# Attention with a cumulative bias and two mixers on one core: queries and keys of batches 1 to 3 split in place instead of through HBM

## The chip, the cores and the metric

The kernel runs on one core of a Trainium2 chip. The metric is the device time of one execution in microseconds (us). TensorE (PE) does the matmuls, VectorE (DVE), ScalarE (ACT) and GpSimd (POOL) work elementwise, SyncE (SP) issues most DMAs; each engine takes its instructions strictly in the order in which they are written, and waits at one whose operands are not there yet.

## The reference, cut to what matters

```python
# q, k, v: (4 batches, 8 heads, 576, 64); s: (4, 8, 576)
scores = q @ k.T / 8
cum    = cumsum(maximum(s, 0))
scores = where(causal, -1e9, scores + minimum(-(cum[:, None] - cum[None, :]), 0))
attn   = softmax(scores)
x      = attn @ v                       # heads side by side: (4, 576, 512)
# mixer 1: two mixes of x with the row before it (mu_k, mu_r)
y      = sigmoid(xr @ w_r) * (relu(xk @ w_k) ** 2 @ w_v)
# mixer 2: over tokens, then over channels
u      = y + (relu(y.T @ w_tok1) @ w_tok2).T
out    = u + relu(u @ w_ch1) @ w_ch2
```

The weights are float64 in memory. Where precision matters, a float32 number is held as a high part (rounded for the fast float32 matmul, `F32R`) and a low part (the rest), and a product is built from high·high, high·low and low·high.

## The kernel before, in words

The 32 (batch, head) pairs are numbered `g`. The eight of batch 0 go a short way: `early` (the first 256 rows) and `late` (the other 320) compute scores in plain float32, beside the conversion of the first weights. The 24 of batches 1 to 3 are the *visits* `i` = 0 to 23. A visit has score tiles `j` of 128 rows; the last 64 rows of an even visit and of the odd one after it share one *joint tile* of 128 rows (`scores` with `pair`), computed with the even visit's `j` = 4 and fed by the X tiles of both. So an even visit has five tiles, an odd one four.

For each tile: PE computes scores (L307, L308), DVE adds the mask and takes the maximum (L278), ACT the exponential and its sum (L289), POOL and DVE the reciprocal (L290, L291), POOL scales the tile (L292), PE transposes it (L435, L450), ACT and DVE split that into high and low (`PF`, `PT`), and PE multiplies with the values (L493).

The scores come from two matmuls of 128 contracted rows. `X1` holds four rows of bias (cumulative sums in parts), zeros, and the high parts of queries and keys in rows 64 to 127; `X2` holds low queries over high keys and high queries over low keys. There are two `X1` and two `X2`, for even and odd visits. `place(i)` fills them when visit `i`-1 begins, by four DMAs from HBM: the bias from `ext_d`, three slices from `hl_d`. The parts in `hl_d` are made two visits (128 partitions) at a time: `load` brings a quarter (queries or keys, 288 columns) into `PB`, `split` takes the high part on ACT (L75), the low part on POOL (L239), and stores both to `hl_d` (L240). `hl_d` has room for all 24 visits, `PB` for two quarters.

The bias parts are made once, at the start, in three column pieces (`split_bias`): POOL writes ones (L197) into a tile `e`, DVE fills the rest (L77, L199, L79), ACT's queue stores it to `ext_d` (L202). The pool `cp` has one buffer for `e`. Batch 0's `late_load` (L371, L372) reads `ext_d` too.

The order of instructions on each engine is laid down when the program is built: every piece of work gets a place in one line by `at(...)`, and a scheduler with a cost model takes what is ready and stands first. Units of the two mixers stand between the attention items, so PE has their matmuls between score tiles. The last 300 us are matmuls of the channel mixer.

Of the kernel before, what the change touches and what calls it, by code (L numbers as in the profile page):

```python
# [8 lines left out]
F32 = mybir.dt.float32  # L9
F32R = mybir.dt.float32r  # L10
# [9 lines left out]
def f32(ap):  # L20
    return ap.bitcast(F32)
# [3 lines left out]
def attention_moe_mixer(  # L25
# [70 lines left out]
    act = {}  # L96

    ext_d = dram.tile([G, 4, 2, S], F32, name="ext_d")
    hl_d = dram.tile([G - H, D, 4, S], F32, name="hl_d")
    y_d = dram.tile([B, DM, S], F32, name="y_d")  # L100
    u_d = dram.tile([B, DM, S], F32, name="u_d")

# [17 lines left out]
        ps_v = att.enter_context(tc.tile_pool(name="ps_v", bufs=1, space=PSUM, reuse_waits="tile"))  # L120

    VS = v_p.tile([128, NS, 2 * D], F32, name="VS")
    maskp = v_p.tile([128, S // 2], BF16, name="maskp")

# [19 lines left out]
    def constants():  # L146
        nc.gpsimd.affine_select(
            out=maskc[:, 512:640], in_=maskc[:, 512:640], pattern=[[-1, 128]],
            compare_op=ALU.is_ge, fill=-8.0e9, base=0, channel_multiplier=1,
        )  # L150
        make_identity(nc, ident)
        nc.gpsimd.memset(maskp, 0.0)
        nc.gpsimd.tensor_copy(maskp[0:TAIL, S // 2 - TAIL:], maskc[0:TAIL, 512:512 + TAIL])
        nc.scalar.dma_start(out=maskp[TAIL:2 * TAIL, S // 2 - TAIL:], in_=maskc[0:TAIL, 512:512 + TAIL])

    def behind(p, cell):
        nc.gpsimd.tensor_copy(cell, xt[0, p][0:1, 1:2])
# [13 lines left out]
    def bias_rows(cp):  # L171
# [14 lines left out]
                copy("D", e32[:, 1, 0, :], cum[:, a:z], -1.0)  # L186
        return cum, e32

    def split_bias(cp, cum, behind):
        n = 3  # L190
        for c in range(n):
            a, z = S * c // n, S * (c + 1) // n
            e = cp.tile([G, 4, 2, z - a], F32R, name="e")
            if c == 0:
                nc.gpsimd.tensor_copy(f32(e[0:1, 0, 1, 0:1]), behind)
            for r, t in ((1, 1), (3, 1), (0, 0), (2, 0)):
                nc.gpsimd.memset(f32(e[:, r, t, :]), 1.0)  # L197
            copy("D", e[:, 0, 1, :], cum[:, a:z])
            nc.vector.tensor_tensor(out=e[:, 2, 1, :], in0=cum[:, a:z], in1=f32(e[:, 0, 1, :]), op=ALU.subtract)  # L199
            for x in (0, 2):  # L200
                copy("D", e[:, x + 1, 0, :], f32(e[:, x, 1, :]), -1.0)
            nc.scalar.dma_start(out=ext_d[:, :, :, a:z], in_=f32(e))  # L202
# [10 lines left out]
    def xs(i):  # L213
        return X1[i % 2], X2[i % 2]

    qk_raw = {}

    def stage():
        if "PB" not in act:
            act["PB"] = qk_p.tile([128, 8 * QC], F32, tag="HX", name="PB")  # L220
        return act["PB"]

    def part(y):
        x, c = divmod(y, 2)
        return x, S * c // 2, S * (c + 1) // 2

    def load(i, y):
        g = visits[i][0]
        x, c0, c1 = part(y)
        t = qk_raw[i, y] = stage()[:, y % 2 * S // 2:(y % 2 + 1) * S // 2]  # L230
        nc.sync.dma_start(out=t, in_=qk[g:g + 2, :, x, c0:c1].rearrange("h d s -> (h d) s"))

    def split(i, y):
        g = visits[i][0] - H
        x, c0, c1 = part(y)
        t = qk_raw.pop((i, y))
        e = stage()[:, S + y % 2 * S:S + y % 2 * S + S].rearrange("p (t s) -> p t s", t=2)
        copy("A", e[:, 1].bitcast(F32R), t)
        nc.gpsimd.tensor_tensor(out=e[:, 0], in0=t, in1=e[:, 1], op=ALU.subtract)  # L239
        nc.sync.dma_start(out=hl_d[g:g + 2, :, 2 * x:2 * x + 2, c0:c1].rearrange("h d t s -> (h d) t s"), in_=e)  # L240

    def load_v(i):
        b, h = divmod(visits[i][0], H)
# [15 lines left out]

    def place(i):  # L260
        g = visits[i][0]
        t = hl_d[g - H]
        if i < 2:
            X2[i] = x_tile(2 + i, F32R)
        x1, x2 = xs(i)
        nc.sync.dma_start(out=f32(x1[0:4]), in_=ext_d[g])
        nc.sync.dma_start(out=f32(x1[64:128]), in_=t[:, 1:4:2])
        nc.sync.dma_start(out=f32(x2[0:64]), in_=t[:, 0:4:3])
        nc.sync.dma_start(out=f32(x2[64:128]), in_=t[:, 1:3])

    pst = {}

# [21 lines left out]
    def scores(i, j):  # L294
        pair = j == NS - 1
        w = 128 * j + (TAIL if pair else 128)
        m = 128
        q0 = 128 * j
        P = p_p.tile([128, w], F32, tag=f"P{j}", name=f"P{j}")
        mx = st_p.tile([128, 2], F32, tag="mx", name="mx")  # L300
        parts = [(0, w // 2), (w // 2, w)] if pair else [(0, w)]
        for x, (c0, c1) in enumerate(parts):
            ps = ps_s.tile([128, 512], F32, tag="s", name="s")
            for e in (1, 0) if pair else (0,):
                x1, x2 = xs(i + e)
                n, a = (TAIL * (1 + e), S - TAIL * (1 + e)) if pair else (128, q0)
                nc.tensor.matmul(ps[0:n, 0:c1 - c0], x1[:, 0, a:a + n], x1[:, 1, c0:c1], start=True, stop=False)  # L307
                nc.tensor.matmul(ps[0:n, 0:c1 - c0], x2[:, 0, a:a + n], x2[:, 1, c0:c1], start=False, stop=True)  # L308
            softmax_max(j, ps, P, mx, x, c0, c1, None if not pair else maskp if x else maskc[:, 0:c1])
        softmax(j, P, mx, x, pair)  # L310
        pst[i, j] = P
# [20 lines left out]
    def early(h, j, V0, cp):  # L332
# [6 lines left out]
        softmax_max(j, ps, P, mx, 0, 0, w)  # L339
        softmax(j, P, mx, 0)  # L340
        if h == 0 and j == 0:
            with at(2):
                split_bias(cp, cum, P[0:1, 0:1])
        if j == 0:
            pt[0] = ps_t.tile([128, 512], F32, tag="t", name="t")
# [299 lines left out]
    def attention_item(n):  # L645
        if n < N1:
# [4 lines left out]
            if j == 2 and h > 1 and h % 2 == 0 and h // 2 + 1 < H // 2:  # L651
                with at(N0 + n):
                    late_values(h // 2 + 1)
            if h >= H - 4:
                x = 3 * (h - H + 4) + j - 2
                with at(N0 + n + 0.1):
                    if x >= 4 and x < 8:
                        split(0, x - 4)
                    if x in (2, 3, 4, 5):
                        load(0, x - 2)  # L660
                    if x == 8:
                        load_v(0)
                    if x in (10, 11):
                        load(2, x - 10)
            if h == H - 1 and j == 3:
                with at(N0 + n + 0.2):
                    split_v(0)
            if h == H - 2 and j == 2:
                with at(N0 + n):
                    for x in range(2):  # L670
                        X1[x] = x_tile(x, F32R)
                        nc.gpsimd.memset(f32(X1[x][0:64]), 0.0)
            if h == H - 1 and j == 2:
                with at(N0 + n):
                    place(0)
# [8 lines left out]
        if j == 0 and i + 1 < len(visits):  # L684
            with at(N0 + n):
                place(i + 1)
        if i % 2 == 0:
            with at(N0 + n + 0.1):
                if j < 4 and i + 2 < len(visits):
                    split(i + 2, j)  # L690
                    if j < 2:
                        load(i + 2, 2 + j)
                if j == NS - 1 and i + 2 < len(visits):
                    load_v(i + 2)
        else:
            with at(N0 + n + 0.1):
                if 2 <= j < 4 and i + 3 < len(visits):
                    load(i + 3, j - 2)
            if j == 1 and i + 1 < len(visits):
                with at(N0 + n + 0.2):  # L700
                    split_v(i + 1)
        with at(N0 + n):
            scores(i, j)
        with at(N0 + n + 1.5):
# [37 lines left out]

    act["mt"], act["mtb"], act["mtw"] = cp, 1, QC
    constants()
    with at(3):
        mixes()
    for h in range(H):
# [276 lines left out]
```

## Time and profile before

| | us |
|---|---|
| median of the runs (lowest, highest of 3) | 874.16 (873.43, 876.98) |
| the profiled execution | 872.61 |
| its span, first to last instruction | 870.8 |
| PE busy in the span | 840.6 (97%) |
| DVE, ACT, POOL busy | 485.1, 452.6, 343.4 |
| moved by DMA | 108.36 MB |

Matmul records overlap (one lasts about 0.3 us and the next starts 0.1 to 0.2 us after it), so a busy PE is not one at its peak; its waits, and the starts of successive matmuls, tell what it loses. Idle time of another engine counts only where PE waits for its result. Stretches are named by their bounds in us from the span's start.

### The profile page before, as it was taken

The page shows a single profiled execution, that of the slowest core. Times are in us where ns is not written, and L with a number is a line of the kernel's source. Part 1 is how long each engine was busy: PE and PEld are TensorE (multiplying, and loading weights), DVE is VectorE, ACT ScalarE, POOL GpSimd, SP SyncE. Part 2 cuts the span into 40 slices and gives each one's busy share as a digit, 9 for nine tenths or more (in the row PEclk, how much of TensorE's full clock was granted, in tenths as well). Part 3 has the DMA queues.
Part 4 walks back from the last instruction along what each step waited for, and adds up shares of the span by engine and source line. Part 5 has one row for each costly group of instructions (what it writes and reads, how often), then busy time and mean ns, then how long its engine had stood idle before and what let it go on. Part 6 is the DMA issues. An engine that isn't in the chain of part 4 may idle for free. (4 is left out here: it accounts for less than half of the span.)

```text
span 870.8 us, 17455 instructions
## 1 busy us (share of the span) xinstructions
PE 840.6 (97%) x6127; PEld 790.5 (91%) x6127; DVE 485.1 (56%) x1352; ACT 452.6 (52%) x1257; POOL 343.4 (39%) x601
## 2 busy tenths in 40 slices
PE   8889998999899999999999999999999999999998
PEld 5656777988789999999999989999999999999998
DVE  5797776565879566985469757951331222222221
ACT  4688766865886656868377865840310221211210
POOL 4565666864785544645256854720000000000000
PEclk9899999999999999999999999999999999999999
DMA  7943778687974244431234746553021112112100
GB/s 191 266 134 88 199 218 230 192 240 210 252 204 133 70 111 117 100 93 41 83 94 129 230 143 217 177 181 94 7 92 54 44 31 74 42 32 73 38 25 26
DMA packets 88024, 108.36 MB, mean 124 GB/s; under 512 B 11152, under 2 KB 71568, under 8 KB 87936
## 3 DMA queue, kind: packets, MB, share of 16 engines
q1 hardware_dynamic: 81408, 91.56, 37.7%
q0 software_dynamic: 4576, 15.08, 5.5%
q8 instruction: 49, 0.80, 0.4%
q10 hardware_dynamic: 1952, 0.60, 0.3%
q14 instruction: 39, 0.32, 0.1%
HBM read 77.74 MB, written 28.90 MB: 122 GB/s over the span
## 5 line engine op out<-in xcount | busy, mean ns | idle before, releaser
L863 ACT ACTIVATE HID<-c 128x256 fp32r<-128x256 f32 (+1 forms) x96 | 39.3, 410 | 220.9 <-PE c L108 220.8
L108 PE MATMUL vd<-KK,WV 128*128 128x256 f32 (+1 forms) x768 | 120.9, 300 | 0.1
L108 PEld LDWEIGHTS vd<-KK,WV 128*128 128x128 f32 x768 | 106.6, 188 | 2.4 <-issue 0.9
L292 POOL TENSOR_SCALAR P<-P,sum 128x128 f32<-128x128 f32 (+4 forms) x148 | 93.6, 636 | 36.2 <-DVE sum L291 30.2
L108 PE MATMUL h<-XK,WK 128*128 128x320 f32 (+1 forms) x672 | 105.9, 303 | 0.7 <-DVE XK L517 0.5
L108 PE MATMUL c<-HID,WV 128*128 128x256 f32 (+1 forms) x768 | 104.9, 291 | 0.0
L108 PE MATMUL c<-U,WK 128*128 128x256 f32 (+1 forms) x768 | 103.2, 291 | 1.4 <-DVE HID L864 1.4
L289 ACT ACTIVATE P<-P,mx 128x128 f32<-128x128 f32 (+4 forms) x148 | 86.9, 588 | 30.3 <-DVE mx L278 23.0
L108 PEld LDWEIGHTS c<-HID,WV 128*128 128x128 f32 x768 | 100.6, 188 | 0.0
L108 PEld LDWEIGHTS c<-U,WK 128*128 128x128 f32 x768 | 98.6, 188 | 1.7 <-DVE HID L864 1.7
L108 PEld LDWEIGHTS h<-XK,WK 128*128 128x128 f32 x672 | 93.8, 189 | 2.1 <-DVE XK L517 0.7
L864 DVE SCALAR_TENSOR_TENSOR HID<-c,HID 128x256 fp32r<-128x256 f32 (+1 forms) x96 | 43.8, 456 | 81.1 <-ACT HID L863 81.0
L278 DVE CUSTOM_DVE_ANT_0 P<-s,maskc 128x128 f32<-128x128 f32 (+4 forms) x148 | 69.1, 478 | 22.1 <-PE t L435 8.4
L928 DVE TENSOR_TENSOR ut<-c,ut 128x256 f32<-128x256 f32 (+1 forms) x32 | 14.6, 458 | 119.3 <-PE c L108 112.0
L529 POOL TENSOR_TENSOR KK<-k,KK 128x256 fp32r<-128x256 f32 (+1 forms) x64 | 55.8, 877 | 19.8 <-ACT k L528 18.7
L108 PE MATMUL r<-XR,WR 128*128 128x320 f32 (+1 forms) x384 | 60.0, 299 | 0.0
L290 POOL TENSOR_SCALAR sum<-sum 128x1 f32<-128x1 f32 (+1 forms) x148 | 32.4, 219 | 67.6 <-ACT P L289 57.2
L108 PE MATMUL c<-HID,WR 128*128 128x256 f32 (+1 forms) x384 | 54.8, 291 | 0.0
L108 PEld LDWEIGHTS r<-XR,WR 128*128 128x128 f32 x384 | 52.8, 188 | 1.1 <-ACT raw L614 0.4
L108 PE MATMUL c<-U,C1A 128*128 128x256 f32 (+1 forms) x384 | 52.8, 296 | 0.1
L108 PEld LDWEIGHTS c<-U,C1A 128*128 128x128 f32 x384 | 51.5, 190 | 0.3 <-ACT U L913 0.3
L108 PEld LDWEIGHTS c<-HID,WR 128*128 128x128 f32 x384 | 51.3, 188 | 0.0
(133 smaller groups left out, 1658.4 us busy)
## 6 DMA issues: line engine op xcount, KB each, us to landing
X<-hl_d SPq DMA_DIRECT2D x72, 288.0 KB
hl_d<-PB SPq DMA_DIRECT2D x48, 288.0 KB
raw<-in_moe_w_ch_dram POOLq DMA_DIRECT2D x48, 256.0 KB, 3.3
PB<-in_qk_dram SPq DMA_DIRECT2D x48, 144.0 KB
yt<-y_d SPq DMA_DIRECT2D x16, 288.0 KB
u_d<-yt SPq DMA_DIRECT2D x16, 288.0 KB
raw<-in_moe_w_k_dram SPq DMA_DIRECT2D x8, 512.0 KB
raw<-in_moe_w_v_dram SPq DMA_DIRECT2D x16, 256.0 KB
```

Of the source, the lines that this page charges most:

```text
L108: nc.tensor.matmul(ps, a, b, start=first and i == 0, stop=last and i == n - 1)
L278: nc.vector.tensor_tensor_reduce(out=P[0:m, c0:c1], in0=ps[0:m, 0:c1 - c0], in1=mask[0:m], scale=-scale, scalar=3.0e38 if x == 0 else mx[0 ...
L289: nc.scalar.activation(out=P[0:m, 0:w], in_=P[0:m, 0:w], func=AF.Exp, bias=mx[0:m, x:x + 1], scale=-1.0, accum_out=sm[0:m, 0:1])
L290: nc.gpsimd.tensor_scalar(out=sm[0:m, 0:1], in0=sm[0:m, 0:1], scalar1=1e-9, scalar2=1.0, op0=ALU.add, op1=ALU.mult)
L292: nc.gpsimd.tensor_scalar(out=P[0:m, 0:w], in0=P[0:m, 0:w], scalar1=sm[0:m, 1:2], scalar2=1.0, op0=ALU.mult, op1=ALU.mult)
L529: nc.gpsimd.tensor_tensor(out=kk[:, 1, m, 0:n], in0=t[:, 0:n], in1=f32(kk[:, 0, m, 0:n]), op=ALU.subtract)
L863: nc.scalar.activation(out=hi, in_=ps, func=AF.Relu)
L864: nc.vector.scalar_tensor_tensor(out=lo, in0=ps, scalar=0.0, in1=f32(hi), op0=ALU.max, op1=ALU.subtract)
L928: nc.vector.tensor_tensor(out=t, in0=ps, in1=t, op=ALU.add)
```

## The change

`hl_d` and `PB` go. `load(i)` brings queries and keys of one visit (64 partitions by 2 by 576) into a half of a tile `RQ`, the even visits into the lower 64 partitions, the odd ones into the upper; `sides(i)` says which. `place(i)` then makes all parts where they are used: for keys, then queries, ACT writes the high part into `X1`, a DMA copies it within SBUF to its place in `X2`, and POOL writes the low part into `X2` in two halves of 288 columns. It ends with the load for visit `i`+2. For odd visits the halves of X are exchanged, so that ACT and POOL stay in the same partitions.

The joint tile's columns are cut at 512 (512 and 64) instead of 288 and 288, and its mask has 64 columns. The three bias pieces get three homes (two in the tiles that later hold transposed scores, one in `cp`), their ones are written by `bias_ones` among the first instructions, and `split_bias` stands earlier in the line (`at(4)`).

```diff
-    maskp = v_p.tile([128, S // 2], BF16, name="maskp")
+    maskp = v_p.tile([128, TAIL], BF16, name="maskp")
...
+    def bias_ones(cp, n):
+        for c in range(n):
+            w = S // n
+            e = pt_tile(c, F32R)[0:G, 0:8 * w] if c < 2 else cp.tile([G, 8 * w], F32R, name="e")
+            e = e.rearrange("g (r t s) -> g r t s", r=4, t=2)
+            for r, t in ((1, 1), (3, 1), (0, 0), (2, 0)):
+                nc.gpsimd.memset(f32(e[:, r, t, :]), 1.0)
+            ones.append(e)
...
     def split_bias(cp, cum, behind):
-        n = 3
+        n = len(ones)
         for c in range(n):
             a, z = S * c // n, S * (c + 1) // n
-            e = cp.tile([G, 4, 2, z - a], F32R, name="e")
-            if c == 0:
-                nc.gpsimd.tensor_copy(f32(e[0:1, 0, 1, 0:1]), behind)
-            for r, t in ((1, 1), (3, 1), (0, 0), (2, 0)):
-                nc.gpsimd.memset(f32(e[:, r, t, :]), 1.0)
+            e = ones[c]
+            nc.gpsimd.tensor_copy(f32(e[0:1, 0, 1, 0:1]), behind)
...
+    def sides(i):
+        a, z = slice(0, D), slice(D, 2 * D)
+        return (a, z) if i % 2 == 0 else (z, a)
+
+    def raw_qk():
+        if "RQ" not in act:
+            act["RQ"] = qk_p.tile([128, 8 * QC], F32, tag="HX", name="RQ")
+        return act["RQ"][:, 0:2 * S].rearrange("p (t s) -> p t s", t=2)
+
+    def load(i):
+        nc.sync.dma_start(out=raw_qk()[sides(i)[0]], in_=qk[visits[i][0]])
...
     def place(i):
...
-        nc.sync.dma_start(out=f32(x1[0:4]), in_=ext_d[g])
-        nc.sync.dma_start(out=f32(x1[64:128]), in_=t[:, 1:4:2])
-        nc.sync.dma_start(out=f32(x2[0:64]), in_=t[:, 0:4:3])
-        nc.sync.dma_start(out=f32(x2[64:128]), in_=t[:, 1:3])
+        a, z = sides(i)
+        rq = raw_qk()[a]
+        nc.sync.dma_start(out=f32(x1[z][0:4]), in_=ext_d[g])
+        for y in (1, 0):
+            nc.scalar.activation(out=x1[a, y], in_=rq[:, y], func=AF.Copy)
+            high, low = (z, a) if y else (a, z)
+            nc.sync.dma_start(out=f32(x2[high, y]), in_=f32(x1[a, y]))
+            for c in range(2):
+                cs = slice(S * c // 2, S * (c + 1) // 2)
+                nc.gpsimd.tensor_tensor(out=x2[low, y, cs], in0=rq[:, y, cs], in1=f32(x1[a, y, cs]), op=ALU.subtract)
+        if i + 2 < len(visits):
+            load(i + 2)
...
-        parts = [(0, w // 2), (w // 2, w)] if pair else [(0, w)]
+        parts = [(0, 128 * j), (128 * j, w)] if pair else [(0, w)]
...
-            with at(2):
+            with at(4):
                 split_bias(cp, cum, P[0:1, 0:1])
```

The program's order moves with it. On POOL, at the start, the bias pieces' ones (`L197`, into `e`) stood between the first softmax tiles `P` and the first weights `WK`:

```order
L290 TENSOR_SCALAR sum<-sum 128x1
L197 MEMSET e 32x192 x4
L292 TENSOR_SCALAR P_288<-P_288,sum 128x128
L290 TENSOR_SCALAR sum<-sum 128x1
L621 TENSOR_TENSOR WK<-raw,WK 128x4x128
L292 TENSOR_SCALAR P_305<-P_305,sum 128x256
L290 TENSOR_SCALAR sum<-sum 128x1
L292 TENSOR_SCALAR P_327<-P_327,sum 128x128
L290 TENSOR_SCALAR sum<-sum 128x1
L292 TENSOR_SCALAR P_344<-P_344,sum 128x256
L197 MEMSET e 32x192 x4
```

In the changed kernel POOL reaches the same tiles with the ones long written (they are among its first rows), and only three one-element copies (L204) stand between the first tiles:

```order
L290 TENSOR_SCALAR sum<-sum 128x1
L292 TENSOR_SCALAR P_179<-P_179,sum 128x128
L290 TENSOR_SCALAR sum<-sum 128x1
L204 COPY PT_161<-P_179 1x1
L204 COPY PT_166<-P_179 1x1
L204 COPY e<-P_179 1x1
L290 TENSOR_SCALAR sum<-sum 128x1
L292 TENSOR_SCALAR P_214<-P_214,sum 128x256
L290 TENSOR_SCALAR sum<-sum 128x1
L292 TENSOR_SCALAR P_248<-P_248,sum 128x128
```

So no write of ones waits for a store of `e` in the middle of the softmax rows any more. Next, POOL at the first visits, before: single subtractions for `PB` (later visits' parts) stand between the scalings of the score tiles `P` of visits 0 and 1:

```order
L292 TENSOR_SCALAR P_1727<-P_1727,sum 128x128
L239 TENSOR_TENSOR PB<-PB 128x288
L290 TENSOR_SCALAR sum<-sum 128x1
L239 TENSOR_TENSOR PB<-PB 128x288
L290 TENSOR_SCALAR sum<-sum 128x1
L292 TENSOR_SCALAR P_1744<-P_1744,sum 128x256
L292 TENSOR_SCALAR P_1791<-P_1791,sum 128x384
L290 TENSOR_SCALAR sum<-sum 128x1
L292 TENSOR_SCALAR P_1831<-P_1831,sum 128x512
L239 TENSOR_TENSOR PB<-PB 128x288
```

In the changed kernel the same place has four subtractions together, into the `X2` of the next even visit, right behind the tiles of visit 0:

```order
L292 TENSOR_SCALAR P_1777<-P_1777,sum 128x384
L290 TENSOR_SCALAR sum<-sum 128x1
L292 TENSOR_SCALAR P_1814<-P_1814,sum 128x512
L267 TENSOR_TENSOR X_1563<-RQ,X_1459 64x288 x4
L251 TENSOR_TENSOR VV_1922<-VS,VV_1922 128x2x128
L290 TENSOR_SCALAR sum<-sum 128x1
L251 TENSOR_TENSOR VV_1922<-VS,VV_1922 128x3x128
L290 TENSOR_SCALAR sum<-sum 128x1
L267 TENSOR_TENSOR X_1709<-RQ,X_1461 64x288 x4
```

The subtractions now belong to the visit that needs them next, and come in blocks of four. Last, PE at the joint tile of visits 8 and 9 (`X_1469`, `X_1471` are the two `X1` before, `X_1576`, `X_1718` the two `X2`); before:

```order
L307 MATMUL s<-X_1471 128x288
L308 MATMUL s<-X_1718 128x288
L307 MATMUL s<-X_1469 64x288
L308 MATMUL s<-X_1576 64x288
L307 MATMUL s<-X_1471 128x288
L308 MATMUL s<-X_1718 128x288
L307 MATMUL s<-X_1469 64x288
L308 MATMUL s<-X_1576 64x288
```

and in the changed kernel (`X_1461` and `X_1709` belong to the odd visit, `X_1459` and `X_1563` to the even one):

```order
L307 MATMUL s<-X_1461 128x512
L308 MATMUL s<-X_1709 128x512
L307 MATMUL s<-X_1459 64x512
L308 MATMUL s<-X_1563 64x512
L435 MATMUL t<-ident,P_2888 128x128 x3
L493 MATMUL pv<-PF,VV_1922 128x256 x2
L493 MATMUL pv<-PF,VV_1922 128x128 x2
L435 MATMUL t<-ident,P_2923 128x128 x4
L307 MATMUL s<-X_1461 128x64
L308 MATMUL s<-X_1709 128x64
L307 MATMUL s<-X_1459 64x64
L308 MATMUL s<-X_1563 64x64
```

Four matmuls of 512 columns and four of 64 take the place of eight of 288.

## Rows read from the trace of the kernel before

**Rows 1.** Windows: us; PE, PEld, DVE, ACT, POOL busy (x); clock; DMA share; GB/s.

```profile
0.00:61.50 61.50, 52.43 (x285) 37.42 (x285) 43.91 (x132) 41.53 (x104) 34.40 (x75) 0.92 0.78 198
128.90:260.00 131.10, 119.81 (x829) 109.73 (x828) 87.60 (x299) 94.97 (x272) 89.78 (x168) 0.99 0.81 223
140.00:160.00 20.00, 17.58 (x109) 15.78 (x108) 12.58 (x43) 14.52 (x42) 14.12 (x26) 0.91 0.82 214
260.00:420.00 160.00, 159.92 (x1222) 157.79 (x1221) 116.18 (x364) 112.61 (x307) 84.34 (x161) 1.00 0.35 91
```

**Rows 2.** Waits of PE, 128.9:260 (total us, times, longest); then the longest, timeline.

```profile
PE s L308 <- DMA X<-hl_d: 4.1, 3, 2.3
...
147.07 0.30 PE L308 MATMUL s<-X 128*128 128x128 f32 x1 [2.31 <-DMA X<-hl_d]
```

**Rows 3.** Waits of ACT and of POOL, 128.9:260.

```profile
ACT PB L75 <- DMA PB<-in_qk_dram: 25.6, 17, 3.6
...
POOL PB L239 <- ACT PB L75: 16.5, 12, 3.2
```

**Rows 4.** DMA issues, 128.9:260 (count, KB each).

```profile
DMA packets 23739, 29.21 MB, mean 223 GB/s; under 512 B 2116, under 2 KB 19780, under 8 KB 23723
...
X<-hl_d SPq DMA_DIRECT2D x36, 288.0 KB
hl_d<-PB SPq DMA_DIRECT2D x34, 288.0 KB
PB<-in_qk_dram SPq DMA_DIRECT2D x34, 144.0 KB
```

**Rows 5.** Timeline of the start (start us, us, instruction, [idle before <-releaser]).

```profile
27.05 0.25 DVE L77 CAST e<-st 32x192 fp32r<-32x192 f32 x1 [2.02 <-DMA ext_d<-e]
...
27.14 0.95 POOL L197 MEMSET e<- 32x192 f32 x4 [3.40 <-DMA ext_d<-e]
...
33.12 0.40 ACT L289 ACTIVATE P<-P,mx 128x128 f32<-128x128 f32 x1 [4.00 <-DVE t L514]
```

**Rows 6.** Timeline of PE at a joint tile and behind it.

```profile
225.77 0.39 PE L308 MATMUL s<-X 128*128 128x512 f32 x1
226.00 0.29 PE L307 MATMUL s<-X 128*128 128x288 f32 x1
...
227.05 0.60 PE L435 MATMUL t<-ident,P 128*128 128x128 f32 x4
...
231.76 0.81 PE L435 MATMUL t<-ident,P 128*128 128x128 f32 x5
232.32 1.38 PE L493 MATMUL pv<-PT,VV 128*128 128x320 f32 x9
233.54 0.31 PE L307 MATMUL s<-X 128*128 128x128 f32 x1
```

**Rows 7.** Groups by shape: busy us, mean ns.

```profile
L239 POOL TENSOR_TENSOR PB<-PB 128x288 f32<-128x288 f32 x48 | 40.0, 835 | 23.9 <-ACT PB L75 18.6 <-DMA y_d<-e 3.7 <-DVE sum L291 0.6
L75 ACT ACTIVATE PB<-PB 128x288 fp32r<-128x288 f32 x48 | 21.2, 441 | 30.7 <-DMA PB<-in_qk_dram 29.8 <-POOL PB L239 0.3 <-issue 0.2
L75 ACT ACTIVATE WK<-raw 128x512 fp32r<-128x512 f32 x8 | 5.4, 677 | 1.3 <-DVE raw L616 1.3
L289 ACT ACTIVATE P<-P,mx 128x576 f32<-128x576 f32 x12 | 9.3, 773 | 4.9 <-DVE mx L278 4.7
L292 POOL TENSOR_SCALAR P<-P,sum 128x576 f32<-128x576 f32 x12 | 10.3, 856 | 1.9 <-DVE sum L291 1.8
L292 POOL TENSOR_SCALAR P<-P,sum 64x576 f32<-64x576 f32 x8 | 6.8, 846 | 3.0 <-DVE sum L291 2.9
```

**Rows 8.** DMA issues, whole span: median us from issue to landing.

```profile
raw<-in_moe_w_ch_dram POOLq DMA_DIRECT2D x48, 256.0 KB, 3.3
...
raw<-in_moe_w_tok_dram POOLq DMA_DIRECT2D x2, 128.0 KB, 2.6
```

**Rows 9.** Instructions on the tile PB: ns min/median/max, first and last start.

```profile
L239 POOL TENSOR_TENSOR PB<-PB x48: 788/810/1083, 91.3 to 267.4; 128x288 f32<-128x288 f32 x48
```

More of the change, by code (lines that the diff above doesn't have):

```diff
@@ L98, in attention_moe_mixer @@
     ext_d = dram.tile([G, 4, 2, S], F32, name="ext_d")
-    hl_d = dram.tile([G - H, D, 4, S], F32, name="hl_d")
     y_d = dram.tile([B, DM, S], F32, name="y_d")
@@ L152, in constants @@
         nc.gpsimd.memset(maskp, 0.0)
-        nc.gpsimd.tensor_copy(maskp[0:TAIL, S // 2 - TAIL:], maskc[0:TAIL, 512:512 + TAIL])
-        nc.scalar.dma_start(out=maskp[TAIL:2 * TAIL, S // 2 - TAIL:], in_=maskc[0:TAIL, 512:512 + TAIL])
+        nc.gpsimd.tensor_copy(maskp[0:TAIL], maskc[0:TAIL, 512:512 + TAIL])
+        nc.scalar.dma_start(out=maskp[TAIL:2 * TAIL], in_=maskc[0:TAIL, 512:512 + TAIL])
     def behind(p, cell):
@@ L187, in bias_rows @@
         return cum, e32
+    def bias_ones(cp, n):
[6 more added lines that the diff above has]
+            ones.append(e)
+    ones = []
     def split_bias(cp, cum, behind):
-        n = 3
+        n = len(ones)
         for c in range(n):
             a, z = S * c // n, S * (c + 1) // n
-            e = cp.tile([G, 4, 2, z - a], F32R, name="e")
-            if c == 0:
-                nc.gpsimd.tensor_copy(f32(e[0:1, 0, 1, 0:1]), behind)
-            for r, t in ((1, 1), (3, 1), (0, 0), (2, 0)):
-                nc.gpsimd.memset(f32(e[:, r, t, :]), 1.0)
+            e = ones[c]
+            nc.gpsimd.tensor_copy(f32(e[0:1, 0, 1, 0:1]), behind)
             copy("D", e[:, 0, 1, :], cum[:, a:z])
@@ L214, in xs @@
         return X1[i % 2], X2[i % 2]
[L216 to L240, printed above, removed]
+    def sides(i):
[7 more added lines that the diff above has]
+        nc.sync.dma_start(out=raw_qk()[sides(i)[0]], in_=qk[visits[i][0]])
     def load_v(i):
@@ L261, in place @@
         g = visits[i][0]
-        t = hl_d[g - H]
         if i < 2:
@@ L653, in attention_item @@
                     late_values(h // 2 + 1)
-            if h >= H - 4:
-                x = 3 * (h - H + 4) + j - 2
+            if h == H - 3 and j == 2:
                 with at(N0 + n + 0.1):
[L657 to L664, printed above, removed]
+                    load(0)
+                    load(1)
+            if h == H - 2 and j == 4:
+                with at(N0 + n + 0.1):
+                    load_v(0)
             if h == H - 1 and j == 3:
@@ L671, in attention_item @@
                         X1[x] = x_tile(x, F32R)
-                        nc.gpsimd.memset(f32(X1[x][0:64]), 0.0)
+                        nc.gpsimd.memset(f32(X1[x][sides(x)[1]]), 0.0)
             if h == H - 1 and j == 2:
@@ L686, in attention_item @@
                 place(i + 1)
-        if i % 2 == 0:
+        if i % 2 == 0 and j == NS - 1 and i + 2 < len(visits):
             with at(N0 + n + 0.1):
[L689 to L701, printed above, removed]
+                load_v(i + 2)
+        if i % 2 and j == 1 and i + 1 < len(visits):
+            with at(N0 + n + 0.2):
+                split_v(i + 1)
         with at(N0 + n):
@@ L744, in attention_moe_mixer @@
     constants()
+    bias_ones(cp, 3)
     with at(3):
```

## The prediction

> **What bounds the kernel now.** I read the busy time by stretches first. In the last 300 us and in most of the middle the starts of PE's matmuls follow one another without a gap; 260 to 420 is such a stretch: PE is idle for 0.08 of 160 us [rows 1]. There an edit helps only if it takes matmuls away, and this one doesn't. Two stretches are different. The start, 0 to 61.5, ends when the first conversions and batch 0 are done; its PE work is partly filler, so its length is set by DVE, ACT, POOL and the DMAs of the first weights (share 0.78 [rows 1]). And in 128.9 to 260, where about the first half of the visits lies, PE is busy for 119.81 of 131.10 us: it loses 11.3 us [rows 1].
>
> The views of waits say what ends those losses. 4.1 us in three waits are the second score matmul (L308) waiting for parts from `hl_d`; the longest, 2.31, ends at 147.07 [rows 2]. The window around it, 140 to 160, has a mean granted clock of 0.91 against 1.00 in 260 to 420 [rows 1]: the clock stood for part of it at 1.2 GHz instead of 2.4, after PE had been idle, and 0.09 × 20 = 1.8 us went with that. The other 7.2 us of the loss are many short waits of PE on DVE, ACT and POOL. Behind them stand longer ones: ACT waits 25.6 us for `PB` to arrive (17 times), and POOL 16.5 us for ACT's high part of it (12 times) [rows 3]. While ACT stands at L75, the exponentials behind it stand too. The DMAs behind that are 34 loads of 144 KB, 34 stores of 288 KB and 36 reloads of 288 KB, 25.7 of the 29.21 MB of the stretch [rows 4], at a DMA share of 0.81 [rows 1].
>
> **The start.** Before, the single buffer `e` makes DVE wait 2.02 and POOL 3.40 us for the store to `ext_d`, with four ones-writes of 0.95 behind it on POOL; ACT's next exponential begins only after 4.00 us of idleness [rows 5]. With three homes and early ones all this goes. Not all of ACT's 4.00 reaches the end of the start, since weights and ACT's conversions wait for DMAs too. Bounds: 0 (the weights set the end) and −5 (all of ACT's wait, and a ones-write of 0.95 more). I take −3.0, nearer to ACT's row, because the softmax items of batch 0 are one chain through ACT, DVE and POOL.
>
> **The reloads.** X no longer comes from `hl_d`: −4.1 of waits, and −1.8 of clock if nothing takes their place. I take −5.9; the smaller end is −2, if other waits keep the clock low and half of the idle time stays.
>
> **The other waits of that stretch.** ACT and POOL lose the waits at the head of their queue. The new ACT copies read a tile `RQ` loaded two visits ahead, and the stretch's traffic falls to 29.2 − 25.7 + 12 visits × (288 + 2 × 144 KB, 7.1 MB) = 10.6 MB, so the share to about 0.3. Bounds −7.2 and 0; I take half, −3.5, since half of PE's 7.2 is the plain latency of the softmax chain, which the change leaves alone.
>
> **The new chain of a visit.** A copy of 64 × 576 on ACT has no row. 128 × 288 takes 441 ns and 128 × 512 takes 677 [rows 7], which makes 0.74 at 576 columns; 64 partitions instead of 128 save nothing (846 against 856 ns on POOL at 576 columns [rows 7]). Four subtractions take 4 × 0.835 = 3.34 [rows 7]. A DMA within SBUF has no row either; 128 KB land 2.6 us after issue and 256 KB after 3.3 [rows 8], so 144 KB take about 2.7. From the moment the places in X are free, keys' copy 0.74, then POOL's 3.34 from there (queries' copy lies beside it) and some 0.8 of hand-over: 4.9 us. The DMA path, 0.74 × 2 + 2.7 + 0.4 = 4.6, lies beside that.
>
> What is there to hold it? At visits 8 and 9 the joint tile's matmuls end with the first transposes at 227.05, and the next even visit's matmul starts at 233.54 [rows 6]: a window of 6.5, less some 0.2 until the last matmul is drained. So 4.9 fits. But place's instructions stand in their queue behind what is there: with one exponential (0.77), one scaling (0.86) and one 0.835 of another unit ahead [rows 7], it is 7.4, 1.1 us late. Before, a reload of 288 KB was late at three visits [rows 2]. For odd visits the window is longer, as four of five tiles lie in it. I take 1.1 late at about half of the six even visits of the stretch: +3. Bounds: 0, if POOL is free each time, and +11, if 1.8 is lost at each of six. Behind a late subtraction on POOL stand the scalings, then PE's transposes.
>
> **Joint tiles.** Before, eight matmuls of 288 columns start from 226.00 to 227.05, 0.131 each. 512 columns take 0.23 (225.77 to 226.00), and small ones, by the five transposes from 231.76 to 232.32, 0.112 each [rows 6]. If a 64-column one is bound by its weight load as these are, the new tile takes 4 × 0.23 + 4 × 0.112 = 1.37 against 1.05; if it is bound by columns, 4 × 0.23 + 4 × 0.03 = 1.04. I take 1.26, so +0.21 for each of 12, +2.5. Bounds 0 and +3.8.
>
> **More work on POOL and ACT.** POOL has 96 subtractions instead of 48 (+40 us), ACT 48 copies of 0.74 for 48 of 0.441 (+14) [rows 7], as 64 partitions are done at a time. In 128.9 to 260 POOL comes to 89.8 − 34 × 0.835 + 48 × 0.835 = 101.5 of 131, ACT to 95.0 − 15.0 + 17.9 = 97.9. In 260 to 420, where nearly all splits were already done, POOL goes from 84.3 to about 118 of 160 and ACT from 112.6 to about 127 [rows 1]. That PE was idle for 0.08 there shows slack of unknown depth. Bounds 0 and +8 (a loss per time as in the stretch before); I take +2. The cover is the mixer units between score tiles; if it is gone, rival 2 has the price.
>
> **Sum.** −3.0 − 5.9 − 3.5 + 3 + 2.5 + 2 = −4.9. From the profiled execution's 872.6 that is 867.7; the median of the runs, 874.16, lies 1.55 above that execution, so 869.3.
>
> **Rivals.**
>
> 1. The stretch becomes as smooth as 260 to 420. For it speaks that there, with loads and splits nearly over and the share at 0.35, PE lost 0.08 [rows 1]; against it, that in that stretch POOL had a third less to do. −3 − 11.3 − 1.8 + 2.5 = −13.6, so 860.5.
>
> 2. The split is late at every even visit. Mechanism: place(i) can't start until the even X is free, at the end of the joint tile, and its four subtractions end last; the even visit's L308 waits, and PE's order lets nothing past it. At 1.5 late for 11 placed even visits it costs 16.5 and the clock's 1.8 comes back, on top of the joint tiles' 2.5, while start and reloads give −3 − 5.9: 872.6 + 11.9, so with the 1.55 some 886 (884 to 886 as the lows come out). It decides from 0.7 us per even visit: the forecast's sum without its +3 is −7.9, and 7.9 / 11 = 0.7 takes all of it; from (7.9 + 4.4) / 11 = 1.1 the kernel is slower by more than noise. For it speaks the small margin of 6.3 over 4.9, against it that mixer units can be ordered ahead of the score tile. What POOL's instructions cost beside a busy DVE bears on this: L239 ran 48 times with 788 at least, 810 as the median and 1083 ns at most [rows 9], so a wait for DVE was 0.27 us at worst. The Trainium skill ("SBUF — State Buffer", section "Who interferes with whom") says that a DVE instruction with two SBUF inputs and a GpSimd one that reads SBUF shut each other out for the whole instruction, which speaks against twice as many subtractions; by that rule four of them could be 4 × 0.27 = 1.1 us later (an estimate from rows 9). The trace shows it at few of the 48, as the median lies 22 ns above the least.
>
> 3. Nothing is left. The start's end is set by the first weights' DMAs (share 0.78 [rows 1]), which is unchanged, so its −3 goes; and late splits eat what the reloads gave. −5.9 − 3.5 + 3 + 2.5 + 2 and 3 more of late splits = +1, some 875.
>
> **How the numbers follow.** Forecast 0.45, rival 1 0.20, rival 2 0.20, rival 3 0.15. About 0.5% (4.4 us) is what a measurement of this kernel can tell from no change: faster means below 869.8, slower above 878.5. The forecast's own range is 865 to 875, just over half of it below 869.8 by its terms' bounds; with rival 1 that makes 0.44 faster. Rival 2 and a thin end of the forecast give 0.22 slower, the rest, with rival 3, 0.34. The range: 860 takes in most of rival 1 (its better half lies beyond), 882 the half of rival 2 with lateness near 1.1; some 0.2 stay outside.
>
> **What would show it.** The first `h` matmuls 3 us earlier and no wait of DVE or POOL on `ext_d<-e`: the start. No releaser `hl_d` in PE's waits and a clock of 1.00 from 140 to 160: the reloads. ACT's 25.6 gone and PE's loss in the stretch of the visits near 6: the other waits. PE waiting at L308 on POOL's L267 for about 1 us at some even visits: the chain; at all of them: rival 2. Starts of the 64-column matmuls 0.03 or 0.11 apart: the joint tile. The forecast is wrong if the stretch's loss stays above 11 us, or if 260 to 420 shows idle time of PE of several us.

## The result: slower by 0.8%, and the profile after

The changed kernel takes 883.12 us (median of 7 runs, 879.6 to 886.7) against 876.27 of the kernel before on the same chip (7 runs, 873.43 to 878.11). The ratio is 1.0083 with a 95% interval of 1.0061 to 1.0105. That is slower, and above the predicted range. The profiled execution took 883.61 us, its span is 881.8.

The stretches of the changed kernel, in the columns of [rows 1] (length; busy us and count of PE, PEld, DVE, ACT and POOL; granted clock; DMA share; GB/s):

```profile
0.00:61.50 61.50, 49.96 (x289) 35.47 (x289) 42.91 (x129) 40.97 (x101) 35.30 (x80) 0.97 0.83 203
60.00:75.00 15.00, 11.52 (x45) 7.03 (x44) 12.23 (x29) 9.69 (x26) 7.73 (x10) 0.66 0.18 54
128.90:260.00 131.10, 122.07 (x831) 110.22 (x830) 88.18 (x288) 96.98 (x255) 99.17 (x175) 0.97 0.31 77
140.00:160.00 20.00, 16.68 (x96) 13.67 (x95) 11.15 (x33) 13.23 (x32) 16.11 (x26) 0.91 0.31 78
260.00:420.00 160.00, 156.31 (x1179) 151.12 (x1178) 119.69 (x355) 120.08 (x319) 121.55 (x204) 1.00 0.25 66
```

Read three things in it. The DMA share of 128.9 to 260 fell as forecast (0.81 to 0.31). POOL's busy time rose as forecast, to 99 and 122. But PE, idle for 0.08 us in 260 to 420 before, now loses 3.69 there, and the clock is low in a place where it was not before, at 60 to 75 (0.66; 1.00 before). Equal windows do not hold quite the same work: the first score matmul of a visit starts at 135.2, where it started at 128.8 before.

Where PE waits now, over the whole span (us in total, times, longest):

```profile
PE pv L360 <- ACT T L75: 5.3, 3, 2.7
PE s L307 <- DVE mx L278: 5.2, 7, 2.4
PE s L392 <- DVE mx L278: 4.9, 2, 3.5
```

No wait on `hl_d` is left; the waits of [rows 2] are gone. In their place score matmuls (L307 of the visits, L392 of batch 0) wait for DVE's maximum of an earlier tile, which has to free a score buffer; the waits at L360 belong to the start. The longest on a visit ends at 152.55, almost where the old one ended (147.07). The timeline around it:

```profile
149.41 3.56 POOL L267 TENSOR_TENSOR X<-RQ,X 64x288 fp32r<-64x288 f32 x4 [0.97 <-ACT X L262]
...
149.54 2.02 DVE L515 SCALAR_TENSOR_TENSOR t<-xt,omu,t 128x320 f32<-128x320 f32 x2
...
151.82 0.67 DVE L278 CUSTOM_DVE_ANT_0 P<-s,maskc 128x512 f32<-128x512 f32 x1
...
152.55 0.44 PE L307 MATMUL s<-X 128*128 128x384 f32 x1 [2.38 <-DVE mx L278]
```

While POOL runs its four subtractions for the next visit, two instructions of DVE take 2.02 us together. One of this shape takes 0.54 elsewhere in the same trace (383.06, below). PE stands for 2.38 us until the maximum behind them is there. About 1 us of that is the slowness of the two; the rest is the plain order of DVE's instructions (the same place without POOL's reads is shown below, with the fill).

```profile
383.06 0.54 DVE L515 SCALAR_TENSOR_TENSOR t<-xt,omu,t 128x320 f32<-128x320 f32 x1
```

To count such losses I took windows of 5 us from 60 to 610 in each trace, and summed PE's idle time and, for the clock, 5 us times what the granted clock lacks to 1.00. Before: 17.8 idle and 1.7 clock. After: 22.1 and 8.6. The two make 11.2 us more, and the span is 11.0 longer. So the lower clock behind the waits is the larger part in these windows of this execution. The start, which they leave out, went the other way: its clock rose from 0.92 to 0.97, and PE's idle time in 0 to 61.5 from 9.07 to 11.54. The medians, 6.9 us apart, say that this pair of executions shows more than the usual difference.

### The profile page after: what moved, and what is told of

Same layout as the page of the kernel before. It is cut to its first block, busy times and chain, and to the rows that moved or that the text cites. A ratio compares the mean times of both kernels' runs of the same rounds, so it can differ in the third digit from the quotient of the medians.

```text
span 881.8 us, 17430 instructions
## 1 busy us (share of the span) xinstructions
PE 846.1 (96%) x6127; PEld 790.1 (90%) x6127; DVE 493.0 (56%) x1352; ACT 466.4 (53%) x1257; POOL 386.9 (44%) x651
## 5 line engine op out<-in xcount | busy, mean ns | idle before, releaser
L107 PE MATMUL vd<-KK,WV 128*128 128x256 f32 (+1 forms) x768 | 118.6, 300 | 0.0
L292 POOL TENSOR_SCALAR P<-P,sum 128x128 f32<-128x128 f32 (+4 forms) x148 | 95.4, 650 | 36.7 <-DVE sum L291 28.7
L289 ACT ACTIVATE P<-P,mx 128x128 f32<-128x128 f32 (+4 forms) x148 | 86.6, 586 | 28.7 <-DVE mx L278 24.3
L278 DVE CUSTOM_DVE_ANT_0 P<-s,maskc 128x128 f32<-128x128 f32 (+4 forms) x148 | 72.0, 497 | 38.6 <-PE t L435 20.2
L267 POOL TENSOR_TENSOR X<-RQ,X 64x288 fp32r<-64x288 f32 x96 | 80.8, 860 | 12.6 <-ACT X L262 8.0
L615 DVE SCALAR_TENSOR_TENSOR raw<-raw 128x256 int32<-128x256 int32 (+2 forms) x77 | 39.8, 519 | 22.4 <-ACT raw L614 15.0
```

The source lines that it names most:

```text
L107: nc.tensor.matmul(ps, a, b, start=first and i == 0, stop=last and i == n - 1)
L267: nc.gpsimd.tensor_tensor(out=x2[low, y, cs], in0=rq[:, y, cs], in1=f32(x1[a, y, cs]), op=ALU.subtract)
L278: nc.vector.tensor_tensor_reduce(out=P[0:m, c0:c1], in0=ps[0:m, 0:c1 - c0], in1=mask[0:m], scale=-scale, scalar=3.0e38 if x == 0 else mx[0 ...
L289: nc.scalar.activation(out=P[0:m, 0:w], in_=P[0:m, 0:w], func=AF.Exp, bias=mx[0:m, x:x + 1], scale=-1.0, accum_out=sm[0:m, 0:1])
L292: nc.gpsimd.tensor_scalar(out=P[0:m, 0:w], in0=P[0:m, 0:w], scalar1=sm[0:m, 1:2], scalar2=1.0, op0=ALU.mult, op1=ALU.mult)
L615: nc.vector.scalar_tensor_tensor(out=low, in0=high, scalar=3, in1=low, op0=ALU.logical_shift_left, op1=ALU.bitwise_or)
```

## The experiments

Each ratio is to the kernel before, run beside it on the same chip. The experiments under "The subtractions on POOL" and "The start and the clock" keep the program's order instruction by instruction: the edit is made after the order has been laid down. All others let the scheduler lay it down anew.

### The parts alone

**The homes** on the kernel before:

```diff
-            e = cp.tile([G, 4, 2, z - a], F32R, name="e")
-            for r, t in ((1, 1), (3, 1), (0, 0), (2, 0)):
-                nc.gpsimd.memset(f32(e[:, r, t, :]), 1.0)
+            e = ones[c]
...
+    bias_ones(cp, 3)
```

> The kernel before with the three homes of the bias pieces alone (early ones, place 4 in the line). Theory 'start' (the new order of the start sends weight pieces later and makes PE wait for DVE near 60 us, after which the clock is at its lower level while the mixer's matmuls begin): 3 to 5 us slower than before, with a wait of PE of over 2 us near 60 and a mean clock under 0.95 in 61.5 to 128.9. Theory of the prediction (the removed waits shorten the start): 3 us faster. If the start's loss comes with the in-place loads instead: within 1 us of before.

Measured: 876.74, ratio 1.0032 (1.0009 to 1.0056). The wait near 60 is there, on DVE (PE at L400 here is L392 of the change):

```profile
PE s L400 <- DVE mx L286: 4.7, 2, 2.9
```

The homes remove the waits of [rows 5] and still do not make the kernel faster; 2 to 3 us slower is what is measured. Both signs that theory "start" named are there (the wait, and a clock of 0.94 in 61.5 to 128.9), but the time is at the lower end of what it asked, or below.

**The joint tiles** on the kernel before:

```diff
-        parts = [(0, w // 2), (w // 2, w)] if pair else [(0, w)]
+        parts = [(0, 128 * j), (128 * j, w)] if pair else [(0, w)]
```

> The kernel before with joint tiles of 512 and 64 columns alone. By the pitches of the trace of after (0.23 for 512, 0.06 for 64 columns) +1.3 us; by the prediction +2.5; a theory that any edit shifts the order of the program and moves the time by several us either way expects something outside 0 to +4.

Measured: 882.03, ratio 1.0083 (1.0067 to 1.0100), outside 0 to +4. In the changed kernel's trace a matmul of 512 columns takes 0.233 us from start to start. Of the four of 64 columns, where they follow one another, the two over 128 rows take 0.03 or 0.11 each, the two over 64 rows 0.058: 0.26 to 0.34 in all. So a tile takes 1.19 to 1.27 against 1.05, and 12 of them 1.7 to 2.7 us. The rest of the 7 us is not in the matmuls. In the profiled execution it lies in 208 to 266, where the clock is 0.88 (first row, joint tiles alone) and was 1.00 before (second row), with a wait of 2.6 us for `hl_d` in it:

```profile
208.00:266.00 58.00, 49.27 (x310) 43.47 (x309) 42.61 (x142) 43.66 (x128) 41.29 (x78) 0.88 0.79 208
```

```profile
208.00:266.00 58.00, 51.40 (x373) 46.79 (x372) 45.12 (x147) 44.95 (x133) 41.96 (x77) 1.00 0.82 225
```

**The in-place splits** alone: the changed kernel with the two edits above taken back.

```diff
...
+            nc.scalar.activation(out=x1[a, y], in_=rq[:, y], func=AF.Copy)
...
+            nc.sync.dma_start(out=f32(x2[high, y]), in_=f32(x1[a, y]))
...
+                nc.gpsimd.tensor_tensor(out=x2[low, y, cs], in0=rq[:, y, cs], in1=f32(x1[a, y, cs]), op=ALU.subtract)
```

> The kernel before with the in-place splits alone (joint tiles of 288 and 288 columns, one buffer for the bias pieces as before). Theory 'blocks on POOL' (four subtractions together hold POOL for 3.3 us and make DVE's instructions wait, so maxima come late): +3 to +6 us, PE idle by 3 us or more in 260 to 420 where before it was idle for 0.08. Theory 'start': the splits cost little, 0 to +2. The prediction's terms: -5.9 - 3.5 + 3 + 2, some 4 us faster.

Measured: 885.88, ratio 1.0126 (1.0106 to 1.0146), more than any theory had. PE loses 4.09 us in 260 to 420, as theory "blocks on POOL" wanted.

**Two parts at a time.** The changed kernel with one home for the bias pieces; the changed kernel with 288 and 288 columns; and the kernel before with homes and joint tiles (the diffs are those above).

> The changed kernel with the bias pieces as before (one buffer, ones behind the stores). Theory 'start': the wait of 3.5 us near 60 and the lower clock behind it go, 879 to 880 (4 us faster than the changed kernel). The prediction's start term: 3 us slower than the changed kernel, 886.

> The changed kernel with joint tiles of 288 and 288 columns. If the joint tiles cost as they did alone: 7 us faster than the changed kernel, 876. By the pitches of the matmuls: 1.3 us faster, 882. If the parts do not add up: anywhere from 880 to 887, as the in-place splits alone took 886.

> The kernel before with the homes and the joint tiles, without the in-place splits. If the parts add up: 875 + 2.8 + 7.3 = 885. If they do not (each part's time is mostly that of the order it brings): 877 to 882.

Measured: 883.17, ratio 1.0081 (1.0057 to 1.0105); 880.97, ratio 1.0071 (1.0037 to 1.0105); 879.79, ratio 1.0058 (1.0035 to 1.0081). The parts do not add up: alone they cost 0.3, 0.8 and 1.3%, together 0.8%. With one home the kernel is as slow as with three, so the wait near 60 does not decide the time: the trace with one home has none longer than 1.2 us in 55 to 75 (the clock in 60 to 75 is 0.77 even so).

**The order alone.** The kernel before with one number changed:

```diff
-            with at(N0 + n + 0.1):
+            with at(N0 + n + 1.0):
                 if j < 4 and i + 2 < len(visits):
                     split(i + 2, j)
```

> The kernel before with one number changed: the splits of an even visit stand 0.9 places later in the line. The work is the same, only the order of the program moves (some 170 rows of PE's order differ). Theory 'order' (any edit that moves the program's order moves the time by several us, through new waits of PE and the lower clock behind them): 3 us or more from before, either way. If the order alone is worth little, within 2 us of before, and then the 7 us of the joint tiles alone are not an accident of the order.

Measured: 877.55, ratio 1.0041 (1.0019 to 1.0064), with no work added. That is about 3 us, between the two expectations. Its profiled execution (882.86, the longest of its nine) has 22.9 us idle and 6.8 clock by the count above. This is one trial, but it shows that some 0.4% can come from the order, which is enough to keep parts that reorder the program from being summed.

### The subtractions on POOL, in a fixed order

**Cut short** in the changed kernel, from visit 2 on; the low parts of the other columns are left out:

```diff
+    def cut(p):
+        return type(p)(ap=[p.ap[0], (1, 32)], offset=p.offset, ...)
...
+                copy.replace(x, ins=[cut(p) for p in x.ins], outs=[cut(p) for p in x.outs]) if x.name in LOWS else x
```

> The changed kernel with its program order kept instruction by instruction; from visit 2 on each subtraction is cut to 32 of 288 columns (low parts of the other columns are left out), so POOL has some 60 us less to do and DVE is not held up by it. Theory 'blocks on POOL': 5 to 7 us faster than the changed kernel, so 876 to 878, with no idle PE in 260 to 420. Theory 'start' or 'order': at most 2 us faster than the changed kernel, 881 or more, the losses stay.

> The changed kernel with its program order kept and its subtractions cut to 144 of 288 columns from visit 2 on (half of the low parts left out), so POOL's subtractions take about 40 us in all, as before. Theory 'POOL's added time' expects most of the 10 us that the cut to 32 columns gave: 875 to 878. Theory 'blocks and order' (their place, not their sum, makes the loss): little of it, 879 to 882.

Measured with 32 columns: 873.08, ratio 0.9988 (0.9969 to 1.0008), 0.95% or 8 us below the changed kernel's 1.0083, more than was expected. With 144 columns: 875.88, ratio 1.0014 (0.9989 to 1.0039), as theory "POOL's added time" expected. What the subtractions take (groups by shape; changed kernel, 144 columns, 32 columns; eight of visits 0 and 1 stay whole and add 6.6 in the last two):

```profile
L267 POOL TENSOR_TENSOR X<-RQ,X 64x288 fp32r<-64x288 f32 x96 | 80.8, 860 | 12.6 <-ACT X L262 8.0 <-PE s L392 1.2 <-DMA VS<-in_v_dram 0.8
```

```profile
L270 POOL TENSOR_TENSOR X<-RQ,X 64x144 fp32r<-64x144 f32 x88 | 45.1, 529 | 12.4 <-ACT X L265 10.1
```

```profile
L270 POOL TENSOR_TENSOR X<-RQ,X 64x32 fp32r<-64x32 f32 x88 | 23.4, 283 | 13.3 <-ACT X L265 11.3
```

And with 32 columns, PE in 260 to 420 is nearly whole again:

```profile
260.00:420.00 160.00, 159.88 (x1218) 156.63 (x1218) 116.79 (x369) 125.23 (x331) 96.94 (x205) 1.00 0.24 64
```

As both programs have one order, their instructions can be lined up one by one (the short kernel's profiled execution took 877.29, 4 us above its median). Its PE draws ahead by 2.4 us between 268 and 280 of the changed kernel's time and by 2.9 between 364 and 388, and stays level between. What stands in the second place, in the changed kernel (one POOL block and the scaling behind it; PE then waits for scalings at 387.81; how the one leads to the other is not shown):

```profile
374.83 4.26 POOL L267 TENSOR_TENSOR X<-RQ,X 64x288 fp32r<-64x288 f32 x4
...
379.20 1.09 POOL L292 TENSOR_SCALAR P<-P,sum 128x384 f32<-128x384 f32 x1
...
387.81 0.44 PE L435 MATMUL t<-ident,P 128*128 128x128 f32 x2 [0.40 <-POOL P L292]
```

**The same cut in the kernel before**, in its own order (single subtractions of 128x288, 48 of them):

> The kernel before with its program order kept; its single subtractions of 128x288 are cut to 32 columns from the second pair of visits on (low parts left out). Theory 'blocks' (dear only as four together at the next visit's need): within 2 us of before, 873 to 876. If POOL's time was as dear before: 5 us or more faster, 870 or less; then the loss of the changed kernel is the time of the 48 added ones alone, block or no block.

Measured: 870.68, ratio 0.9955 (0.9937 to 0.9973). My theory "blocks" falls here: POOL's time was dear before the change too, one subtraction at a time (870 or less was expected of that case; 870.68 just misses it). In [rows 7] they took 40.0 us; in this kernel 12.5 and 3.2:

```profile
L242 POOL TENSOR_TENSOR PB<-PB 128x32 f32<-128x32 f32 x44 | 12.5, 286 | 29.8 <-ACT PB L78 24.6 <-DMA y_d<-e 3.6 <-DVE mx L283 0.5
L242 POOL TENSOR_TENSOR PB<-PB 128x288 f32<-128x288 f32 x4 | 3.2, 800 | 0.1
```

So 24.3 us less on POOL give 0.45%, 3.9 us. In the changed program 80.8 − 51.7 = 29.1 less give 1.0083 − 1.0014, 6.0 us, and 51.7 − 30.0 = 21.7 less give another 2.3. That is 0.16, 0.21 and 0.11 us of the kernel for each us on POOL, each of the three gains uncertain by 2 to 3 us. Between the ratios at 51.7 and 30.0 us, a straight line puts the changed program at 1.000 for 40 us: with as much to do on POOL as before, it takes the time of before, to within some 2 us. All else in the change, gains and losses, comes to about nothing.

That is a balance of two things. By the count of windows above, the profiled execution with 144 columns has 15.8 us idle and 9.3 clock, that with 32 columns 16.7 and 10.2; the kernel before had 17.8 and 1.7. The runs agree: their mean granted clock is 0.986 with 144 and 0.988 with 32 columns, about as in the changed kernel (0.986), against 0.991 of the kernel before beside them. So cutting the subtractions took away idle time and gave little of the clock back.

**Filled instead of subtracted.** POOL writes 864 bytes in each partition and reads nothing:

```diff
...
+        o = type(p)(ap=[(4 * p.ap[0][0], 64), (1, 864)], offset=4 * p.offset, dtype=mybir.dt.uint8, ...)
+        return copy.replace(zero, name=x.name, outs=[o], sync_info=x.sync_info, debug=x.debug)
```

> The changed kernel with its program order kept; from visit 2 on each subtraction is replaced by a POOL fill of 864 bytes per partition, which writes and reads nothing (the low parts are left out). If the fill takes about the 0.8 us of a subtraction: theory 'lock' (the loss comes from DVE instructions that stand while POOL reads) expects nearly the time with the short subtractions, 872 to 877, and DVE's tensor instructions at their least; theory 'occupied POOL' (scalings of score tiles stand behind the block) expects the changed kernel's 880 to 884. If the fill is much shorter than 0.8 us it can't tell the two apart.

```profile
L270 POOL MEMSET X<- 64x864 uint8 x88 | 70.6, 828 | 9.7 <-ACT X L265 7.3 <-DMA VS<-in_v_dram 0.8
```

Measured: 879.03, ratio 1.0045 (1.0029 to 1.0062), at nearly the duration of a subtraction (828 against 860 ns). It lies between both theories. The same DVE instruction in 128.9 to 420, in the changed kernel, with the fill (L520 is L515), and with the short subtractions:

```profile
L515 DVE SCALAR_TENSOR_TENSOR t<-xt,omu,t 128x320 f32<-128x320 f32 x18 | 11.6, 651 | 0.0
```

```profile
L520 DVE SCALAR_TENSOR_TENSOR t<-xt,omu,t 128x320 f32<-128x320 f32 x18 | 10.3, 578 | 0.0
```

```profile
L520 DVE SCALAR_TENSOR_TENSOR t<-xt,omu,t 128x320 f32<-128x320 f32 x19 | 10.5, 554 | 0.0
```

A POOL that only writes holds this instruction up little. At the place of the wait of 2.38 us the trace with the fill has:

```profile
147.61 1.00 DVE L520 SCALAR_TENSOR_TENSOR t<-xt,omu,t 128x320 f32<-128x320 f32 x2
...
149.60 0.44 PE L312 MATMUL s<-X 128*128 128x384 f32 x1 [1.36 <-DVE mx L283]
```

The two instructions take 1.00 us instead of 2.02, and PE waits 1.36 instead of 2.38. With 144 columns they take 1.24 and PE waits 1.60; with 32 columns 1.01 and 1.36. Here the price of POOL's reads reaches PE one to one, and 1.36 us of the wait stay without them. About 3 of the 8 us (1.0083 to 1.0045) therefore go with POOL's reads, and about 5 (1.0045 to 0.9988) with POOL being occupied, which I read as scalings and sums that come late; the first two intervals just overlap, and the fills take 3.6 us less of POOL than the subtractions, so the split is rough.

### The start and the clock

**More filler** ahead of the wait near 60, in a fixed order, alone and with the short subtractions:

```diff
+            if j == 3:
+                WARM.add(a[1].ins.name)
...
+                if x.name in WARM:
+                    row += [copy.replace(x, name=f"I-{10**8 + k}", sync_info=None) for k in range(24)]
```

> The changed kernel with its program order kept and 24 more filler matmuls (0.11 us each, results unused) on PE ahead of the wait that ends at 63.58, so that PE is not idle there for 3.5 us. Theory 'clock' (some 5 us of the loss are the lower clock behind that idle time): the clock in 60 to 75 stays near 1.00 and the kernel is 3 to 5 us faster than the changed kernel, 878 to 880. If the idle time itself and not the clock is the cost: within 1 us of it, or slower by up to 1.

> The changed kernel in its own order with both edits: subtractions cut to 32 columns from visit 2 on (low parts left out) and 24 more filler matmuls ahead of the wait near 60. With POOL's blocks gone, if the 3 us that the filler saves at the start are kept to the end: 870. If they are lost again to later dips of the clock or waits, as with the filler alone: 873, as with the short subtractions alone.

Measured: 882.90, ratio 1.0083 (1.0057 to 1.0109); and 871.56, ratio 0.9977 (0.9949 to 1.0004). With the filler alone the clock does stay up (0.66 in the changed kernel), and is lost later:

```profile
60.00:75.00 15.00, 14.70 (x97) 10.94 (x95) 11.11 (x32) 10.15 (x30) 8.69 (x11) 1.00 0.17 53
145.00:160.00 15.00, 11.79 (x62) 10.97 (x62) 7.16 (x21) 10.83 (x27) 11.20 (x18) 0.77 0.25 64
230.00:245.00 15.00, 13.23 (x73) 11.86 (x74) 9.77 (x32) 11.69 (x31) 13.89 (x23) 0.77 0.41 100
```

Lined up with the changed kernel, PE is 3.3 us ahead from 76 to 149, 2.8 at 232, and 1.4 at 436: the next waits for DVE, and lower clocks behind them, take more than half of it. Theory "clock" holds for the place and not for the sum. The second pair of kernels differs by 0.0011, 1 us, less than the runs can tell.

### The subtractions on DVE

The changed kernel with DVE making the low parts, and the kernel before with all or every second one on DVE; all parts are computed:

```diff
...
-                nc.gpsimd.tensor_tensor(out=x2[low, y, cs], in0=rq[:, y, cs], in1=f32(x1[a, y, cs]), op=ALU.subtract)
+            nc.vector.tensor_tensor(out=x2[low, y], in0=rq[:, y], in1=f32(x1[a, y]), op=ALU.subtract)
```

```diff
-        nc.gpsimd.tensor_tensor(out=e[:, 0], in0=t, in1=e[:, 1], op=ALU.subtract)
+        nc.vector.tensor_tensor(out=e[:, 0], in0=t, in1=e[:, 1], op=ALU.subtract)
```

> The changed kernel with the low parts made by DVE, one subtraction of 64x576 for each of queries and keys, instead of two on POOL; all parts computed. Theory 'lock' or 'occupied POOL': POOL loses 80 us, DVE gains some 30, 873 to 878. If the loss were the lateness of X's parts alone: 880 or less in any case, since DVE is quicker than POOL. If DVE is short of time instead (88 of 131 busy us in 128.9 to 260), PE waits more for maxima: 883 or more.

> The kernel before with its 48 subtractions of 128x288 on DVE instead of POOL; all parts computed. POOL loses 40 us, DVE gains about 21 (0.43 each). Theory 'POOL's queue': 870 to 873, as with the cut subtractions. Theory 'elementwise work, whichever engine': 875 to 878, since DVE's maxima then stand behind them.

> The kernel before with every second subtraction on DVE, all parts computed. Theory 'POOL's queue': half of the gain of the cut, 872 to 874. Theory 'elementwise work': within 2 us of before or slower.

Measured: 878.66, ratio 1.0044 (1.0024 to 1.0064); 885.81, ratio 1.0121 (1.0086 to 1.0157); 880.10, ratio 1.0052 (1.0028 to 1.0077). The first lies 0.7 us above the range of "lock" and "occupied POOL". The second is slower than both theories had it. The third, 4.8 us above the kernel before, goes with "elementwise work" (within 2 us, or slower). In the second kernel DVE now stands for the split (waits in 128.9 to 260):

```profile
POOL sum L290 <- ACT P L289: 48.7, 28, 9.1
ACT PB L75 <- DMA PB<-in_qk_dram: 31.4, 18, 4.5
DVE PB L239 <- ACT PB L75: 23.6, 15, 3.9
```

POOL's 16.5 us of [rows 3] have become DVE's 23.6, and what stands behind them on DVE are the maxima. These kernels are ordered anew, so the part of order in their 5 and 11 us is open. No version with all parts computed beat the kernel before.

## Why the prediction was wrong, step by step

**More work on POOL and ACT, +2: the step that failed.** The prediction counted POOL's 40 us more rightly, and gave them +2 because POOL was busy for 118 of 160 us and PE before had no idle time there. Measured by cutting in a fixed order, the POOL time added by the change is worth as much as all of the loss, 0.8% or 7 us between 40 and 80.8 us of subtractions. Here a busy share of 0.75 was not slack. Each tile needs POOL twice (sum, scaling) between ACT and PE, and POOL's subtractions can put these back. The kernel before showed it in a single wait of PE for L292 (1.3 us) in 128.9 to 260 and in none in 260 to 420; cutting 24.3 us from it gave 3.9 us.

This term is 5 of the 12 us between the forecast's −4.9 and the measured +7. The other 7 are the gains: all other terms add up to −6.9, and by the straight line above they came to about nothing, as the next paragraphs tell. ACT's 14 us more, the other half of this term, stay in all the cut kernels, and no run prices them alone.

**The new chain of a visit, +3: wrong place.** X comes in time: the only wait of a score matmul for L267 in the changed kernel is one of 0.2 us, of the weight load at L308. Rival 2 had the right sign with this mechanism, which did not happen, so it is chance that its 884 to 886 lies near the 883 measured. Its side remark came nearer. The Trainium skill ("SBUF — State Buffer", section "Who interferes with whom") sets a DVE instruction with two SBUF inputs against a GpSimd one that reads. I weighed it by POOL's longest subtraction and put it aside; the trace of after shows the price on DVE's side (two L515 in 2.02 us at 149.54). By that rule a POOL that only writes leaves such an instruction alone, and the fill agrees: 578 against 651 ns.

**The start, −3: nothing.** The waits on `ext_d<-e` went. PE's waits for POOL's first scalings (L349) fell from 4.3 to 0.9 us, but those for ACT's transposed tiles (L360) rose from 2.0 to 5.3, and the first `h` matmul starts at 50.78 instead of 49.10, not 3 us earlier. Weights and softmax items were ordered anew, and a maximum behind weight conversions on DVE made PE wait for 3.48 us at 63.58, with the clock at 0.66 for the next stretch. The filler shows that even taking this away gains nothing in the end.

**The reloads, −5.9: not kept.** The waits on `hl_d` went. Another of 2.38 ended 5.5 us later than the old one, and 140 to 160 has the clock of before, 0.91.

**The other waits, −3.5.** PE's loss in 128.9 to 260 fell by 2.3 us, from 11.3 to 9.0, waits on `hl_d` included, and the mean clock from 0.99 to 0.97, which takes 0.02 × 131 = 2.6 back. The DMA share fell by 0.5 without giving PE anything that can be seen.

**The joint tiles, +2.5.** 1.7 to 2.7 by the starts of the matmuls: the tile measured 1.19 to 1.27, and 1.26 was taken. The term was right as matmul time. Alone the edit cost 7 us, and taking it out of the changed kernel gave some 1 us (1.0083 to 1.0071), less than the runs can tell; the difference lies in waits and clock, and came with a new order.

**The range.** 882 was the upper end; 883.12 lies beyond it, since the rival behind that end was priced by one mechanism, and the other terms were taken as small gains and losses that add up. The experiments show that here they do not add: gains at one place were taken by the next wait.

## What to carry to other kernels

Price an engine that stands in a chain between two others by its added busy time, even at three quarters busy and with hardly a wait in sight (here 0.1 to 0.2 us of the kernel for each us); the quickest test is to cut its instructions short in an unchanged order. A removed wait counts only if the trace shows what would be next at that place: here DVE's maxima stood ready to take over from the DMA. And where a scheduler lays the order down anew, try an edit that moves only the order before reading a few tenths of a per cent as the worth of a part.

## What was not expected of the hardware

A subtraction on POOL of 64x288 takes 860 ns on average and one of 128x288 835, so splitting by half the partitions doubles the time; 32 columns still take 283, so cutting from 288 to 32 saves two thirds, not eight ninths. PE's clock was low after some waits of PE and not after others: in the changed kernel 2.38 us at 152.55 was followed by it (0.50 in 154 to 156), and so was 3.48 at 63.58, but 2.68 at 41.84 was not (1.00 in 41.8 to 50). And two traces of one program order (the changed kernel and that with more filler) have the lower clock at different places, 215 to 225 and 230 to 245. What decides that is open; no run here was made for it.
